# A token order kept through the gating and undone by the store: one HGRN2 attention and gated MLP kernel

## The chip, the cores and the metric

The kernel runs on one core of a Trainium2 chip. The metric is the device time in microseconds of one execution; the kernel before takes 183.43 us (median of three runs, 183.13 to 183.45). A core has five engines that run side by side, each with its own instruction queue, which it works off in order: TensorE (PE in the profile; PEld is its weight load), VectorE (DVE), ScalarE (ACT), GpSimd (POOL) and SyncE (SP). SP computes nothing here: it issues DMA transfers. The transfers of a core run on 16 DMA engines.

## The reference

Inputs are `q`, `k`, `v` and `f_logit` of shape (4 batches, 8 heads, 768 tokens, 48), and two weight matrices.

```python
f = 1.0 / (1.0 + np.exp(-f_logit))
for t in range(S):                      # 768 tokens, per batch and head a 48 x 48 state
    state = f[:, :, t, :, None] * state + np.einsum('bhd,bhe->bhde', k[:, :, t], v[:, :, t])
    y[:, :, t] = np.einsum('bhd,bhde->bhe', q[:, :, t], state)
x = y.transpose(0, 2, 1, 3).reshape(3072, 384)
h = x @ w_in                            # 384 -> 2048
g = h * np.cos(h)
out = g @ w_out                         # 2048 -> 384, written as 3072 x 384 in float32
```

The recurrence is a gated linear attention; what follows is a plain two-layer MLP whose nonlinearity is h·cos(h).

## The kernel before, in words

**Tokens.** The 3,072 tokens are cut into 12 pairs of 256 tokens (`pair(n)`). A load (`load`, L296) brings one of the four inputs of one pair, 384 KB, so that partition p holds tokens 2p and 2p+1 next to each other, for all 8 heads; the first two pairs load f, k and q in halves of 192 KB. Because of that layout the attention works on even tokens and odd tokens as two groups: in every block of 128 tokens its columns stand as 64 even tokens, then 64 odd ones. The code names the two by `e` and the place within them by `n`.

**Attention of a pair.** ACT makes the logarithm of the gate and its exponentials, PE sums them along the tokens, POOL multiplies q and k with them (`qm`, `km`, L404, the tile `qk`). The products are transposed into `qkt`: for pairs 0 to 4 on PE with a copy behind it, for pairs 5 to 11 by a DMA transpose that SP issues (`tq`, L424, two for a pair). PE then makes the scores (`sc`, L456), DVE masks them (`am`, L461, 128x1024 out of PSUM into bf16), PE forms the state (`ps`, L479) and the outputs (`y` and `yi`, L531), and ACT or DVE copies them into `x` (`xe`, L197), model dimension on the partitions, tokens in the columns, still even then odd in each 128.

**MLP.** It runs in 13 units of tokens: two of 128, then eleven of 256 (`moe(m, t0, T)`). A PSUM tile of 1,024 columns holds 8 blocks of 128 columns; PE fills it from `w_in` and `x` (`h`, L579), ACT takes the cosine into the bf16 tile `co` (L584), and DVE multiplies the two into `g` (`gate`, L561): 48 such instructions of 128x1024. `gate` reads its inputs in their order, and writes each result to the column of its token: column n of the even group goes to 2n, column n of the odd group to 2n+1, so that neighbouring results are written two elements apart. `g` thus has its columns in the order of the tokens. For each 128 tokens PE multiplies `g` with `w_out` (`o`, L595, four steps of four matmuls into one PSUM bank, `g` being the stationary operand, so that its columns become the rows of the result), ACT or DVE copies the 128x384 float32 result into one of four tiles `ot` (L197), and a store takes it to HBM (`out`, L606). There are 24 blocks: 22 stores of 192 KB, and the last two blocks (22 and 23) as two stores of 96 KB each, by columns. All are issued by SP, but for the very last, which ACT issues.

**Order.** What runs where and when is written out by hand in the string `ORDER`: each word is a step, the letter of its engine (T is PE, S ACT, V DVE, G POOL, Y SP) and the buffers that its results take; `emit` issues the steps in this order, and each engine runs its own in it. SP's queue is thus one list of loads, weight loads, transposes and stores; what stands behind a store is not issued before it. Loads of q, k, v and f have three buffers each, `ot` has four: the copy into an `ot` tile waits for the store that last read it.

The store, with its place in `moe`, is

```python
G.step(f"out{r0 // C}{cut}", ("SP", "ACT") if cut else ("SP",), lambda e, oc=oc, r0=r0, c0=c0, c1=c1: eng(
    e).dma_start(out=out[r0:r0 + C, c0:c1] if nc is not None else None, in_=oc.ap), reads=[oc])
```

where `C` is 128 and `out` is the 3072 x 384 result in HBM: partition i of `ot` goes to row r0 + i.

Of the kernel before, what the change touches and what calls it, by code (L numbers as in the profile page):

```python
# [16 lines left out]
C = 128  # L17
# [171 lines left out]
def describe(nc, cpool, ppool, q, k, v, f_logit, moe_w_in, moe_w_out, out):  # L189
# [6 lines left out]
    def copy(e, o, i):  # L196
        (nc.scalar.copy if e == "ACT" else eng(e).tensor_copy)(out=o, in_=i)  # L197
# [358 lines left out]
                e, xg[g].ap, py[g].ap[:, 0:DM].rearrange("p (m n) -> p m n", n=C)), reads=[py[g]], writes=[xg[g]])  # L556

    def gate(gv, ph, co, T):

        o = gv.ap if T == C else gv.ap.rearrange("p f (g t) -> p (f g) t", t=C)  # L560
        nc.vector.tensor_mul(out=o.rearrange("p b (n e) -> p b e n", e=2),  # L561
                             in0=ph.ap.rearrange("p (b e n) -> p b e n", e=2, n=64),
                             in1=co.ap.rearrange("p (b e n) -> p b e n", e=2, n=64))


    def moe(m, t0, T):
        n, at = divmod(t0, 2 * C)
        x, xg = xs[n]
        xw = x if T == 2 * C else xg[at // C]
        gT, F = Val(gS), 1024 // T  # L570
        for j in range(KF // F):
            ph, co = Val(p2), Val(coS)
            for s in range(2):
                def first(e, j=j, s=s, ph=ph):
                    xa = xw.ap if T == 2 * C else xw.ap[:, None]
                    for i in range(s * F // 2, (s + 1) * F // 2):
                        f0 = (j * F + i) * 128
                        for kk in range(KM):
                            nc.tensor.matmul(ph.ap[:, i * T:(i + 1) * T].rearrange("p (g t) -> p g t", t=C),  # L579
                                             lhsT=w_in_bf[:, kk, f0:f0 + 128], rhs=xa[:, :, kk, :], start=(i % (F // 2) == 0 and kk == 0),  # L580
                                             stop=((i + 1) % (F // 2) == 0 and kk == KM - 1))
                G.step(f"h{m}.{j}{s}", ("PE",), first, reads=[xw, w_in_v[(j * F + s * F // 2) // 4]],
                       writes=[ph], sums=True)
            G.step(f"co{m}.{j}", ("ACT",), lambda e, ph=ph, co=co: nc.scalar.activation(  # L584
                out=co.ap, in_=ph.ap, func=AF.Sin, bias=halfpi), reads=[ph], writes=[co], table="S")
            gv = gT.part(lambda a, j=j: a[:, j * F:(j + 1) * F, 0:T])
            G.step(f"g{m}.{j}", ("DVE",), lambda e, ph=ph, co=co, gv=gv: gate(gv, ph, co, T),
                   reads=[ph, co], writes=[gv])
        for i in range(T // C):
            po, ot = Val(p1), Val(otS)  # L590
            r0 = t0 + i * C
            for s in range(4):
                def second(e, i=i, s=s, po=po):
                    for j in range(4 * s, 4 * s + 4):
                        nc.tensor.matmul(po.ap[:, 0:DM], lhsT=gT.ap[:, j, i * C:(i + 1) * C],  # L595
                                         rhs=w_out_bf[:, j, :], start=(po.first and j == 4 * s),
                                         stop=(po.final and j == 4 * s + 3))
                G.step(f"o{r0 // C}.{s}", ("PE",), second,
                       reads=[gT.parts[4 * s // F], w_out_v[s]], writes=[po], sums=True)
            cuts = ((".0", 0, DM // 2), (".1", DM // 2, DM)) if m == len(UNITS) - 1 else (("", 0, DM),)  # L600
            for cut, c0, c1 in cuts:
                oc = ot.part(lambda a, c0=c0, c1=c1: a[:, c0:c1])
                G.step(f"ot{r0 // C}{cut}", ("ACT", "DVE"), lambda e, po=po, oc=oc, c0=c0, c1=c1: copy(
                    e, oc.ap, po.ap[:, c0:c1]), reads=[po], writes=[oc])
                G.step(f"out{r0 // C}{cut}", ("SP", "ACT") if cut else ("SP",), lambda e, oc=oc, r0=r0, c0=c0, c1=c1: eng(
                    e).dma_start(out=out[r0:r0 + C, c0:c1] if nc is not None else None, in_=oc.ap), reads=[oc])  # L606

    for n in range(PAIRS):
        pair(n)
# [1 line left out]
    for m, T in enumerate(UNITS):  # L611
        moe(m, t0, T)
        t0 += T
# [104 lines left out]
```

## Time and profile before

| | |
|---|---|
| median of 3 runs | 183.43 us (183.13 to 183.45) |
| profiled execution | 183.05 us, of which the span of instructions is 181.3 us |
| granted TensorE clock | 0.998 of full speed |
| PE busy | 174.0 us (96% of the span) |
| DVE, ACT, POOL busy | 138.2, 130.7, 109.2 us |
| DMA | 33.93 MB in 72,282 packets |

The span is counted from the first to the last instruction; all places in time below are microseconds from its start. "Busy" is the time in which an engine executes. The DMA rows count packets (a packet is one piece that one of the 16 engines moves), and the share of the 16 engines' time that the packets took. The row of a DMA issue gives the time from SP's issue to the landing of the data. The chain of work that ended last is followed back from the last instruction, at each step to what released it.

### The profile page before, as it was taken

Reading aid. Unit: us, or ns where it says so; the run is one execution under the profiler, and the core shown is the slowest. Engines: PE = TensorE matmul, PEld = TensorE weight load, DVE = VectorE, ACT = ScalarE, POOL = GpSimd, SP = SyncE. Lnnn points to the kernel's source line nnn. Section 1 sums busy time; section 2 is a strip of 40 time slices with the busy share of each in tenths; the row PEclk is TensorE's granted clock in tenths of the full one; section 3 lists DMA queues with packets and bytes.
Section 4 is the critical chain, followed back from the end, with each engine's and each line's share of the span. In section 5 each row is a group of like instructions: output and inputs, shape, how many; then the busy total and the mean of one; then the engine's idle time right before and its main releaser. Section 6 shows DMA issues by size and latency. Waiting matters only on the chain.

```text
span 181.3 us, 5818 instructions
## 1 busy us (share of the span) xinstructions
PE 174.0 (96%) x2464; PEld 124.2 (69%) x2464; DVE 138.2 (76%) x206; ACT 130.7 (72%) x187; POOL 109.2 (60%) x139
## 2 busy tenths in 40 slices
PE   7999788999999999999999999999999999999992
PEld 2555357785677876778657886658788767786661
DVE  5359988898685989897999698689888994466260
ACT  3985988778877999989997899769768452473221
POOL 4229889999969996989755968790799000000000
PEclk9999999999999999999999999999999999999999
DMA  6999999999999945996889999749929400110313
GB/s 141 261 261 263 346 304 318 293 283 281 317 264 241 270 77 128 253 230 133 125 162 317 189 242 253 175 125 244 216 85 197 90 4 0 38 52 4 130 43 130
DMA packets 72282, 33.93 MB, mean 187 GB/s; under 512 B 65344, under 2 KB 70720, under 8 KB 72256
## 3 DMA queue, kind: packets, MB, share of 16 engines
q1 hardware_dynamic: 71584, 33.27, 76.6%
q8 instruction: 19, 0.31, 0.7%
q10 hardware_dynamic: 672, 0.30, 0.6%
q14 instruction: 7, 0.06, 0.1%
HBM read 25.17 MB, written 4.72 MB: 165 GB/s over the span
## 4 chain that ended last, share of the span: by engine, by line
PE 80%; DMA 8%; SPq 5%; DVE 3%; POOL 1%; issue 1%; ACT 1%; POOLq 0%
PE ps L595 35%; PE ps L579 32%; DMA k<-in_k_dram 5%; PE ps L531 5%; SPq L296 3%; PE ps L456 3%; DMA v<-in_v_dram 3%; PE ps L479 2%; DVE g L561 1%; SPq L282 1%; PE ps L435 1%; PE ps L374 1%; DVE am L461 1%; POOL qk L404 1%; POOL k L351 1%
## 5 line engine op out<-in xcount | busy, mean ns | idle before, releaser
L561 DVE TENSOR_TENSOR g<-ps,co 128x1024 bf16<-128x1024 f32 x48 | 61.3, 1311 | 15.8 <-ACT co L584 14.8
L595 PE MATMUL ps<-w_out_bf,g 128*128 128x384 bf16 x384 | 68.9, 326 | 0.0
L579 PE MATMUL ps<-x,w_in_bf 128*128 128x256 bf16 (+1 forms) x624 | 68.2, 264 | 0.6 <-DVE x L197 0.5
L584 ACT ACTIVATE co<-ps,halfpi 128x1024 bf16<-128x1024 f32 x48 | 52.7, 1113 | 20.0 <-PE ps L579 19.8
L579 PEld LDWEIGHTS <-w_in_bf 128*128 128x128 bf16 x624 | 56.3, 98 | 9.3 <-DVE x L197 0.7
L595 PEld LDWEIGHTS <-g 128*128 128x128 bf16 x384 | 36.0, 98 | 21.5 <-issue 0.3
L461 DVE TENSOR_TENSOR am<-ps,pmask 128x1024 bf16<-128x1024 f32 x24 | 28.7, 1218 | 5.0 <-PE ps L456 4.8
L404 POOL TENSOR_TENSOR qk<-k,bi 128x384 bf16<-128x384 f32 x22 | 22.0, 1010 | 5.4 <-ACT bi L391 4.7
L404 POOL TENSOR_TENSOR qk<-q,b 128x384 bf16<-128x384 f32 x21 | 20.9, 1004 | 2.7 <-DVE q L338 2.1
L197 POOL COPY vt<-vb 64x384 bf16<-64x384 bf16 x33 | 16.7, 507 | 1.6
L264 PE MATMUL ps<-zero 128*128 128x512 bf16 x54 | 16.1, 426 | 1.2 <-DVE zero L203 1.2
L503 DVE TENSOR_TENSOR sz<-ps,b 64x192 bf16<-64x192 f32 x40 | 14.1, 353 | 2.5 <-PE ps L479 1.6
L341 POOL TENSOR_TENSOR q<-f,q 128x384 f32<-128x384 f32 x10 | 10.0, 1000 | 8.3 <-DMA q<-in_q_dram 6.1
L363 POOL TENSOR_TENSOR sp<-ls 128x384 bf16<-128x384 f32 x10 | 10.2, 1015 | 7.7 <-ACT ls L333 5.9
L329 ACT ACTIVATE f<-f 128x768 f32<-128x768 f32 (+1 forms) x14 | 10.4, 746 | 4.5 <-DMA f<-in_f_logit_dram 4.4
L351 POOL TENSOR_TENSOR k<-k,f 128x384 f32<-128x384 f32 (+1 forms) x12 | 11.1, 930 | 4.2 <-DMA k<-in_k_dram 4.2
L497 DVE TENSOR_TENSOR ps<-ps,sz 64x192 f32<-64x192 f32 x32 | 11.7, 366 | 1.9 <-PE ps L479 0.8
L197 ACT COPY ot<-ps 128x384 f32<-128x384 f32 (+1 forms) x14 | 6.1, 453 | 8.7 <-PE ps L595 8.7
L197 ACT CAST x<-ps 128x384 bf16<-128x384 f32 x12 | 5.5, 479 | 5.9 <-PE ps L531 5.9
L456 PE MATMUL ps<-qkt 48*64 48x128 bf16 (+1 forms) x304 | 8.7, 219 | 1.0 <-DVE sz L503 0.8
L197 DVE CAST x<-ps 128x384 bf16<-128x384 f32 x12 | 6.4, 552 | 4.0 <-PE ps L531 3.8
L264 PEld LDWEIGHTS <-zero 128*128 128x128 bf16 x54 | 4.9, 105 | 6.1 <-issue 2.2
(64 smaller groups left out, 167.5 us busy)
## 6 DMA issues: line engine op xcount, KB each, us to landing
v<-in_v_dram SPq DMA_DIRECT2D x12, 384.0 KB, 6.0
out_dram<-ot SPq DMA_DIRECT2D x22, 192.0 KB, 2.1
f<-in_f_logit_dram SPq DMA_DIRECT2D x10, 384.0 KB, 6.0
k<-in_k_dram SPq DMA_DIRECT2D x10, 384.0 KB, 6.7
q<-in_q_dram SPq DMA_DIRECT2D x10, 384.0 KB, 6.7
g<-in_moe_w_in_dram SPq DMA_DIRECT2D x4, 768.0 KB, 7.6
g<-in_moe_w_out_dram SPq DMA_DIRECT2D x4, 768.0 KB, 5.8
k<-in_k_dram SPq DMA_DIRECT2D x4, 192.0 KB, 4.5
```

Of the source, the lines that this page charges most:

```text
L197: (nc.scalar.copy if e == "ACT" else eng(e).tensor_copy)(out=o, in_=i)
L264: G.step(f"zf{i}", ("PE",), lambda e, dump=dump: nc.tensor.matmul(dump.ap, lhsT=zero[:, 0:128], rhs=zero, start=True, stop=True), writes=[ ...
L351: eng(e).tensor_mul(out=w.ap[:, :, 0, :], in0=w.ap[:, :, 0, :], in1=t.ap[:, :, 0, :])
L404: G.step(f"{nm}{n}.{u}", ("POOL", "DVE") if cut else ("POOL",), lambda e, u=u, j=j, src=src, dec=dec: eng(e).tensor_mul(out=qkp[u][j].ap[: ...
L456: nc.tensor.matmul(o[t0:t1, r, 2 * a + g, :].rearrange("p (e n) -> p e n", e=2), lhsT=wide[s, t0 // 64, :] if turned else wide[s].rearrang ...
L461: G.step(f"am{n}.{u}", ("DVE",), lambda e, u=u, sc=sc: nc.vector.tensor_mul(out=am[u].ap.rearrange("p r b n -> p (r b) n"), in0=sc.ap.rear ...
L497: nc.vector.tensor_add(out=view()[s], in0=view()[s], in1=S0.ap[s, :, r, :])
L503: eng(e).tensor_mul(out=new.ap[s, :, r, :].rearrange("p (u a) n -> p u a n", u=2), in0=view()[s].rearrange("p (u a) n -> p u a n", u=2), i ...
L561: nc.vector.tensor_mul(out=o.rearrange("p b (n e) -> p b e n", e=2), in0=ph.ap.rearrange("p (b e n) -> p b e n", e=2, n=64), in1=co.ap.rea ...
L579: nc.tensor.matmul(ph.ap[:, i * T:(i + 1) * T].rearrange("p (g t) -> p g t", t=C), lhsT=w_in_bf[:, kk, f0:f0 + 128], rhs=xa[:, :, kk, :], ...
L584: G.step(f"co{m}.{j}", ("ACT",), lambda e, ph=ph, co=co: nc.scalar.activation(out=co.ap, in_=ph.ap, func=AF.Sin, bias=halfpi), reads=[ph], ...
L595: nc.tensor.matmul(po.ap[:, 0:DM], lhsT=gT.ap[:, j, i * C:(i + 1) * C], rhs=w_out_bf[:, j, :], start=(po.first and j == 4 * s), stop=(po.f ...
```

## The change

The gating no longer reorders: it writes its columns in the order in which it reads them, so that `g` holds, in each block of 128 columns, 64 even tokens and then 64 odd ones. The rows of `o`, and the partitions of `ot`, then stand in that order, and the store puts them in place: partition 64·e + n of `ot` goes to row r0 + 2n + e. Its destination is written as a pattern of three dimensions, two groups of 64 rows, each row two rows on from the last. The order of the steps, their engines and their buffers are the same.

```diff
     def gate(gv, ph, co, T):
-
-        o = gv.ap if T == C else gv.ap.rearrange("p f (g t) -> p (f g) t", t=C)
-        nc.vector.tensor_mul(out=o.rearrange("p b (n e) -> p b e n", e=2),
-                             in0=ph.ap.rearrange("p (b e n) -> p b e n", e=2, n=64),
-                             in1=co.ap.rearrange("p (b e n) -> p b e n", e=2, n=64))
+        nc.vector.tensor_mul(out=gv.ap if T == C else gv.ap.rearrange("p f (g t) -> p (f g) t", t=C),
+                             in0=ph.ap.rearrange("p (b t) -> p b t", t=C), in1=co.ap.rearrange("p (b t) -> p b t", t=C))
...
                 G.step(f"out{r0 // C}{cut}", ("SP", "ACT") if cut else ("SP",), lambda e, oc=oc, r0=r0, c0=c0, c1=c1: eng(
-                    e).dma_start(out=out[r0:r0 + C, c0:c1] if nc is not None else None, in_=oc.ap), reads=[oc])
+                    e).dma_start(out=out[r0:r0 + C, c0:c1].rearrange("(n e) m -> e n m", e=2) if nc is not None else None, in_=oc.ap), reads=[oc])
```

In the built program one thing changes on DVE's list of instructions, the output pattern of the 48 gates, and one on SP's and ACT's, the destination of the stores (the line numbers move by three):

```
-L606 DMACopy out_dram<-ot_155 128x384
+L603 DMACopy out_dram<-ot_155 2x64x384
...
-L606 DMACopy out_dram<-ot_154 128x192
+L603 DMACopy out_dram<-ot_154 2x64x192
```

## The prediction

> **What bounds the kernel now.** I read the page first (busy shares, DMA, chain), then the windows, which split the span where the loads end.
>
> ```profile
> span 181.3 us, 5818 instructions
> ...
> PE 174.0 (96%) x2464; PEld 124.2 (69%) x2464; DVE 138.2 (76%) x206; ACT 130.7 (72%) x187; POOL 109.2 (60%) x139
> ...
> DMA  6999999999999945996889999749929400110313
> ...
> q1 hardware_dynamic: 71584, 33.27, 76.6%
> ...
> PE 80%; DMA 8%; SPq 5%; DVE 3%; POOL 1%; issue 1%; ACT 1%; POOLq 0%
> ```
>
> ```profile
> core 0: us, PE busy (x) PEld busy (x) DVE busy (x) ACT busy (x) POOL busy (x), PEclk, DMA share, GB/s
> ...
> 60.50:143.80 83.30, 83.30 (x1303) 62.74 (x1302) 72.92 (x98) 71.09 (x98) 62.45 (x78) 1.00 0.84 186
> 143.80:157.30 13.50, 13.50 (x225) 9.62 (x223) 8.91 (x11) 4.55 (x8) 0.00 (x0) 1.00 0.01 2
> 157.30:178.20 20.90, 20.71 (x150) 14.38 (x147) 10.93 (x12) 8.22 (x10) 0.00 (x0) 1.00 0.19 69
> 178.20:181.30 3.10, 0.00 (x0) 0.00 (x0) 0.00 (x0) 0.39 (x2) 0.00 (x0) 0.89 0.34 114
> ```
>
> PE is the bound: it holds 80% of the chain and is busy without a gap from 60.5 (the first store) to 157.3. But DMA is a close second: q1, which carries SP's transfers, keeps 16 engines busy for 76.6% of the span, and 0.84 of them in the stretch of 60.5 to 143.8, the last in which anything is loaded or transposed. That figure is a mean over 16 engines, and holds for each only while every transfer is dealt evenly. After 143.8 there are only stores.
>
> **The gate.** It writes contiguous results instead of results two elements apart. The nearest contiguous write is the mask `am`: same engine, size and types.
>
> ```profile
> L561 DVE TENSOR_TENSOR g<-ps,co 128x1024 bf16<-128x1024 f32 x48 | 61.3, 1311 | 15.8 <-ACT co L584 14.8
> L461 DVE TENSOR_TENSOR am<-ps,pmask 128x1024 bf16<-128x1024 f32 x24 | 28.7, 1218 | 5.0 <-PE ps L456 4.8
> ```
>
> ```profile
> 28.10 1.33 DVE g L561
> ...
> 30.64 1.23 DVE g L561
> ```
>
> So a gate saves between nothing (1311 ns stays) and 1311 − 1218 = 93 ns; I take 93, the row that differs least from what it becomes. That is 48 × 93 ns = 4.5 us of DVE, which has idle time anyway. Only two gates lie on the chain of work: −0.2 us. PE reads `g` as before, in the same blocks of 128 columns: nothing.
>
> **The store's issue.** Its pattern has one more dimension. The least a store's issue took is 0.36 us (ACT row, below), the dearest kind of issue on SP is a transpose (3.31 us for two, below). So 25 issues on SP and one on ACT may grow by between nothing and 1.3 us. On SP this hides behind the stores' own backlog; only the last issue is on the path. I take +0.3 us, near the plain store, since a store it remains.
>
> **The store's transfer.** This is where I see the cost. A view of the DMA between 157 and 160, when two stores run and nothing else:
>
> ```profile
> DMA  0000000000000003699999520000005999999400
> ...
> DMA packets 288, 0.39 MB, mean 131 GB/s; under 512 B 32, under 2 KB 288, under 8 KB 288
> ...
> q1 hardware_dynamic: 288, 0.39, 34.9%
> ...
> out_dram<-ot SPq DMA_DIRECT2D x2, 192.0 KB, 1.9
> ```
>
> Each store is 128 packets of 1,536 bytes (its rows) and 16 short ones, one for each engine. The packets take 34.9% of 16 × 3 us = 16.75 us for 393,216 bytes: 23.5 bytes per ns and engine. On 16 engines a store's 8 packets for each last 12,288 / 23.5 = 0.52 us. The rest of the 1.9 us to landing is fixed: about 0.7 us ahead (issue at 157.33, the busy digits start near 158.05) and 0.65 behind.
>
> In the changed program the destination's outermost dimension is 2, where every copy before has 128 (the instruction lists under the change). If engines are dealt along that dimension, a store has two shares of 64 rows: 98,304 / 23.5 = 4.2 us on each of two engines, 3.7 us more than now, and 2.1 us for a half store (+1.85). If the rows are dealt as before, it is nothing. No transfer of before has a short outermost dimension, so its trace doesn't say which; the 16 equal shares of today fit both. I take two, because that dimension is the one thing of the transfer that the change alters; ends for the range are 0 and 3.7 us.
>
> [...]
>
> **Stage 1, to 60.5:** no store yet; −0.2 us as said.
>
> **Stage 2, 60.5 to 143.8.** What the queue holds:
>
> ```profile
> q1 hardware_dynamic: 39907, 15.30, 83.5%
> ...
> out_dram<-ot SPq DMA_DIRECT2D x15, 192.0 KB, 3.9
> q<-in_q_dram SPq DMA_DIRECT2D x6, 384.0 KB, 5.5
> k<-in_k_dram SPq DMA_DIRECT2D x5, 384.0 KB, 5.0
> v<-in_v_dram SPq DMA_DIRECT2D x5, 384.0 KB, 6.1
> f<-in_f_logit_dram SPq DMA_DIRECT2D x4, 384.0 KB, 5.2
> qkt<-qk SPq DMA_TRANSPOSE x14, 3.3
> ```
>
> Each engine has 83.5% of 83.3 = 69.6 us of work. Part of that is crowding: all packets average 27.9 ns here, while between 115.3 and 118, a quieter moment, short ones cost 48.8% × 16 × 2.7 us / 920 = 22.9 ns:
>
> ```profile
> q1 hardware_dynamic: 920, 0.35, 48.8%
> ```
>
> At that price the (39,907 − 15 × 128) / 16 short packets of an engine are 54.4 us, with 15 × 0.52 for the stores 62 us. Fifteen stores add 15 × 3.7 = 55 us on the two engines: 117 to 125 us of work in a stretch of 83.3. The two engines become the bound, and the last transpose lands 34 to 41 us later (I take 37.5), since a load or transpose has landed only when its slowest engine is through and those two have the stores ahead of it. The engines also idle: before, 83.3 − 69.6 = 13.7 us here. Between 0 (the stores fill the gaps) and 13.7 (they stay, because SP issues in order: a load behind a store waits for PE's results, and PE for the load) I take 5. Queued behind the stores are the loads for POOL and ACT, the transposes for PE's scores, and through the four `ot` buffers PE's own banks.
>
> What the last transpose feeds is not due at once:
>
> ```profile
> 138.55 3.31 SPq L424 DMA_TRANSPOSE qkt<-qk  x2
> 157.33 21.39 SPq L606 DMA_DIRECT2D out_dram<-ot  x10
> ```
>
> ```profile
> 147.65 0.57 PE ps L456 x32
> ```
>
> The last pair's scores start at 147.65, 3.8 us after 143.8: −3.8 us.
>
> **Stage 3, the tail.** The issues of the last stores:
>
> ```profile
> 167.48 1.31 SPq L606 DMA_DIRECT2D out_dram<-ot  x3
> ```
>
> ```profile
> 175.11 3.61 SPq L606 DMA_DIRECT2D out_dram<-ot  x5
> ```
>
> ```profile
> 178.62 0.36 ACTq L606 DMA_DIRECT2D out_dram<-ot  x1
> ```
>
> On two engines the three stores of 167.48 run from 168.2 to 180.8. Block 20 needs the `ot` buffer of block 16, the last of the three: landed 181.4, copied and issued, first packet 182.7. Then two full stores and four halves, 2 × 4.2 + 4 × 2.1 = 16.8 us, to 199.5, landed at 200.1. Today the last lands at 178.62 + 1.7 = 180.3: +19.8 us.
>
> **The sum,** against the profiled execution's 183.05 us (span 181.3 and 1.75 around it; the median of the runs is 0.4 above): 183.05 − 0.2 + 37.5 + 5 − 3.8 + 19.8 + 0.3 = 241.7. I say 242.
>
> **The rivals.**
> Serial: PE's waits come on top of the stores' time instead of beside it. For it: SP's list is in order, and few buffers stand between. Price: all added store time, 22 × 3.7 + 4 × 1.85 = 89 us: 272.
> Tail alone: the loads are early enough for the stores' backlog, and only stage 3 shows: 183 + 20 = 203. Against it: 117 us of work do not fit in 83.3 us. It needs the stores to be cheaper or the stretch's loads to come much earlier.
> Rows dealt as before, on 16 engines: the change leaves the store as it is, and the gates off the path: 183, within 0.2%. For it: the bytes and rows are the same.
> Faster: the same dealing, and the gates' 4.5 us of DVE reach PE. It decides if more than 0.37 us does, four gates on the path where the chain shows two; DVE's share of the chain is 3%, so the price is at most 0.3 to 2 us: about 182.
>
> **How the numbers follow.** Two engines, overlapping: 0.70, between 222 (uncrowded packets, no idle, a cheaper tail) and 262 (crowded, all idle stays). Serial 0.10, 262 to 280. Tail alone 0.10, 200 to 222. As before 0.06. Faster 0.04. The range of 212 to 268 takes the first whole and half of its two neighbours: 0.80. A measurement of this kernel tells 0.2% from no change; slower by more than that holds 0.91 (one in a hundred for dealing as before, with dearer issues), within it 0.05, faster 0.04.
>
> **What would show it.** Gates at about 1,218 ns. A lone store's time to landing at about 5.5 us (0.7 + 4.2 + 0.65) instead of 1.9; two short packets for each store instead of 16, so 26 × 14 = 364 packets fewer in all; the DMA digits at 1 where stores run alone, though DMA is the bound. PE no longer gapless after 60.5, its waits ending with DMA; the chain's DMA share far above 8%. Stores at 2 us would prove the dealing wrong; stores at 5.5 us and PE still gapless, the queueing.

## The result, and the profile after

The changed kernel takes 240.57 us (median of six runs, 239.94 to 242.22) against 183.44 us: 1.3123 times the time before, with a 95% interval of 1.3082 to 1.3165. Ratios, here and below, leave out the runs that lie more than 1.5% above the fastest of their kernel: two of four each for `ot8` and `ot8_free_e4`, one of four for `ot8_e4`, for which the times given are those of the other runs. The profiled execution has a span of 238.2 us, 56.9 us more than before. The page of the kernel after, the lines that answer to those shown of before:

```profile
span 238.2 us, 5818 instructions
...
PE 182.3 (77%) x2464; PEld 127.6 (54%) x2464; DVE 134.5 (56%) x206; ACT 130.8 (55%) x187; POOL 109.3 (46%) x139
...
PEclk9999999999999769999999889999558999997555
DMA  7999999999753587676959585868930001010111
...
DMA packets 71918, 33.93 MB, mean 142 GB/s; under 512 B 64980, under 2 KB 70356, under 8 KB 71892
...
q1 hardware_dynamic: 71234, 33.27, 64.9%
...
DMA 35%; PE 28%; POOL 9%; issue 7%; ACT 6%; SPq 5%; DVE 4%; DVEq 0%; ACTq 0%; POOLq 0%
...
L559 DVE TENSOR_TENSOR g<-ps,co 128x1024 bf16<-128x1024 f32 x48 | 57.2, 1220 | 29.7 <-ACT co L581 28.7
```

The same bytes moved (33.93 MB), in 72,282 − 71,918 = 364 packets fewer: 14 for each of the 26 stores, as forecast with two short packets for a store instead of sixteen. The last ten DMA digits, where stores run alone, stand at 0 and 1: two engines of sixteen are an eighth. DMA has gone from 8% of the chain to 35%, PE from 80% to 28%. The digits of the granted clock, at 9 throughout before, fall to 5 in places.

The rate of the two engines is read from a view of the DMA between 203 and 218, where three stores run alone:

```profile
GB/s 0 0 0 25 12 41 20 33 37 29 41 49 49 49 53 49 49 49 49 53 49 49 49 53 49 49 49 49 53 49 49 53 49 49 49 53 49 33 0 0
DMA packets 390, 0.59 MB, mean 39 GB/s; under 512 B 6, under 2 KB 390, under 8 KB 390
...
q1 hardware_dynamic: 390, 0.59, 11.3%
```

Six short packets for three stores, two each. By the bytes moved, the first store is slow and uneven, and from then on the pair moves 49 to 53 GB/s, by which a store of 196,608 bytes takes 3.9 us. The packets' share gives more: 11.3% of 16 × 15 us = 27.1 us for 589,824 bytes, 21.7 bytes per ns and engine, or 4.5 us for a store. It adds up the packets' times, and packets of one engine overlap: between 209.32 and 213.24, from the end of the first store's packets to the end of the second's, the view shows 13.3% of 16 × 3.92 us = 8.3 us of packet time for two engines, 4.2 us each, within 3.92 us.

```profile
DMA packets 130, 0.20 MB, mean 50 GB/s; under 512 B 2, under 2 KB 130, under 8 KB 130
...
q1 hardware_dynamic: 130, 0.20, 13.3%
```

Where the 56.9 us came from is read at one place in PE's order, the scores of the last pair, the first work on the last transposes. The timeline of PE, before and then after (start, length):

```profile
147.58 0.64 PE L456 MATMUL ps<-qkt 48*64 48x128 bf16 x32
```

```profile
182.33 0.64 PE L456 MATMUL ps<-qkt 48*64 48x128 bf16 x32
```

They start 34.75 us later; the first store is issued at 60.6, as before. From there to the end it is 55.9 us against 33.7: +22.2 us. The longest pieces of the chain of waits in the first of these stretches (60 to 182.4; start, length, what):

```profile
71.49 10.01 DMA out_dram<-ot
102.35 10.45 DMA out_dram<-ot
116.71 7.92 DMA f<-in_f_logit_dram
141.37 7.79 DMA v<-in_v_dram
164.32 11.43 DMA out_dram<-ot
```

Before, this stretch of the chain (60 to 147.7) was all PE:

```profile
by line: PE ps L579 43.4%; PE ps L595 39.6%; PE ps L531 6.6%; PE ps L456 4.5%; PE ps L479 3.0%; PE ps L374 1.5%; PE ps L435 1.0%; PE ps L380 0.5%
```

Now it holds 47.6 us of transfers in five pieces: three stores, and two loads that took 7.9 and 7.8 us to land, where the medians of this stretch were 5.2 and 6.1 before.

### The profile page after: what moved, and what is told of

Same layout as the page of the kernel before. It is cut to its first block, busy times and chain, and to the rows that moved or that the text cites. A ratio compares the mean times of both kernels' runs of the same rounds, so it can differ in the third digit from the quotient of the medians.

```text
span 238.2 us, 5818 instructions
## 1 busy us (share of the span) xinstructions
PE 182.3 (77%) x2464; PEld 127.6 (54%) x2464; DVE 134.5 (56%) x206; ACT 130.8 (55%) x187; POOL 109.3 (46%) x139
## 2 busy tenths in 40 slices
DMA packets 71918, 33.93 MB, mean 142 GB/s; under 512 B 64980, under 2 KB 70356, under 8 KB 71892
## 4 chain that ended last, share of the span: by engine, by line
DMA 35%; PE 28%; POOL 9%; issue 7%; ACT 6%; SPq 5%; DVE 4%; DVEq 0%; ACTq 0%; POOLq 0%
DMA out_dram<-ot 26%; PE ps L576 12%; PE ps L592 11%; DMA v<-in_v_dram 6%; DMA f<-in_f_logit_dram 3%; SPq L296 3%; POOL qk L404 2%; ACT co L581 2%; PE ps L531 2%; POOL vt L197 2%; SPq L603 2%; ACT f L329 1%; POOL sp L363 1%; POOL k L351 1%; ACT ls L333 1%
## 5 line engine op out<-in xcount | busy, mean ns | idle before, releaser
L592 PE MATMUL ps<-w_out_bf,g 128*128 128x384 bf16 x384 | 71.5, 335 | 6.3 <-ACT ot L197 4.3
L559 DVE TENSOR_TENSOR g<-ps,co 128x1024 bf16<-128x1024 f32 x48 | 57.2, 1220 | 29.7 <-ACT co L581 28.7
L576 PE MATMUL ps<-x,w_in_bf 128*128 128x256 bf16 (+1 forms) x624 | 71.9, 272 | 1.8 <-ACT ot L197 1.2
L576 PEld LDWEIGHTS <-w_in_bf 128*128 128x128 bf16 x624 | 58.1, 101 | 12.3 <-issue 2.0
L592 PEld LDWEIGHTS <-g 128*128 128x128 bf16 x384 | 36.9, 100 | 30.1 <-issue 8.2
L461 DVE TENSOR_TENSOR am<-ps,pmask 128x1024 bf16<-128x1024 f32 x24 | 28.7, 1218 | 11.6 <-PE ps L456 11.4
L197 ACT COPY ot<-ps 128x384 f32<-128x384 f32 (+1 forms) x14 | 6.1, 453 | 47.9 <-DMA out_dram<-ot 47.1
L456 PE MATMUL ps<-qkt 48*64 48x128 bf16 (+1 forms) x304 | 9.2, 224 | 14.2 <-DMA qkt<-qk 9.0
L456 PEld LDWEIGHTS <-qkt 48*64 48x64 bf16 (+1 forms) x304 | 6.2, 106 | 17.7 <-DMA qkt<-qk 11.9
L197 DVE COPY ot<-ps 128x384 f32<-128x384 f32 (+1 forms) x12 | 5.8, 518 | 14.9 <-DMA out_dram<-ot 14.1
L479 PE MATMUL ps<-vb,qk 64*64 64x48 bf16 x320 | 6.2, 194 | 5.1 <-ACT bi L395 5.0
```

Source lines behind the costliest of these rows:

```text
L456: nc.tensor.matmul(o[t0:t1, r, 2 * a + g, :].rearrange("p (e n) -> p e n", e=2), lhsT=wide[s, t0 // 64, :] if turned else wide[s].rearrang ...
L461: G.step(f"am{n}.{u}", ("DVE",), lambda e, u=u, sc=sc: nc.vector.tensor_mul(out=am[u].ap.rearrange("p r b n -> p (r b) n"), in0=sc.ap.rear ...
L559: nc.vector.tensor_mul(out=gv.ap if T == C else gv.ap.rearrange("p f (g t) -> p (f g) t", t=C), in0=ph.ap.rearrange("p (b t) -> p b t", t= ...
```

## The experiments

Ratios are to the kernel before, run beside each on the same chip (medians of 183.1 to 183.5 us).

**The two halves of the change, each alone.** `gate_alone`:

```diff
 (after)
-   e).dma_start(out=out[r0:r0 + C, c0:c1].rearrange("(n e) m -> e n m", e=2) ..., in_=oc.ap)
+   e).dma_start(out=out[r0:r0 + C, c0:c1] ..., in_=oc.ap)
```

> The gate writes its columns as it reads them, the store is that of before, so the rows of the result stay in even-then-odd order in HBM. Theory (the cost is the store's alone): gates at 1,220 ns, PE's chain as before, 183.0 to 183.5 us. Rival (the gate's columns cost PE something): over 184 us. Rival (the gates' 4.5 us of DVE reach PE): under 182.5 us.

Measured: 183.0 us, ratio 0.9989 (0.9976 to 1.0001). The gates take 1,219 ns. `store_alone` is the reverse, the gate of before with the store of after:

```diff
 (before)
-   e).dma_start(out=out[r0:r0 + C, c0:c1] ..., in_=oc.ap)
+   e).dma_start(out=out[r0:r0 + C, c0:c1].rearrange("(n e) m -> e n m", e=2) ..., in_=oc.ap)
```

> The gate of before, the store of after, so the rows of the result are permuted. Theory (the store on two engines is the whole cost): 240 to 242 us, as after, with 71,918 DMA packets. Rival (the gate has a part in it): clearly below 240 us.

Measured: 240.84 us, ratio 1.3154 (1.3111 to 1.3196). The whole cost is the store's; what the gate saves, if anything, is at the edge of what the runs tell.

**How many groups.** `store_e16`, `store_e8` and `store_e4` keep the three-dimensional pattern and rows that are apart, and change only the number of groups:

```diff
 (after)
-   ... .rearrange("(n e) m -> e n m", e=2) ...
+   ... .rearrange("(n e) m -> e n m", e=16) ...     # and 8, 4
```

> The kernel after with the destination cut into 16 groups of 8 rows instead of 2 groups of 64: three dimensions and rows that are apart, as after, but an outermost dimension of 16; the rows of the result come out in another order. Theory (the outermost dimension sets the number of engines): 16 engines, 16 short packets a store, 72,282 in all, a lone store lands in about 1.9 us, 183 to 185 us. Rival (the form of the pattern makes the store dear, three dimensions or rows apart, on however many engines): about 240 us.

> The kernel after with 4 groups of 32 rows; the rows of the result come out in another order. Theory: four engines, 2.1 us of a store on each, 26 x 12 = 312 packets fewer than before (71,970). In the middle stretch 15 x 1.6 = 24 us more on four engines: 86 to 93 us of work in 83.3, and a tail of +4.6 us: 187 to 198 us, likeliest 191. Rival (form of the pattern): about 240 us. Rival (time is added in proportion to what a store takes longer, 1.57 of 3.7 us, 42% of 57 us): about 207 us.

> The kernel after with 8 groups of 16 rows (the rows come out in another order): eight engines, 1.05 us of a store on each, half a microsecond more than on sixteen. Sixteen groups cost 1.5 us, four 26.6, two 57. If time grows in proportion to a store's time on its engine (0.52 us more, at about 15.6 us a microsecond, and the 1.5 of the form): 190 to 194 us. If there is a threshold, as the prediction's sum has it (62 to 70 + 15 x 0.52 = 70 to 78 us of work fit in 83, only the tail's 1 to 2 us and the form's 1.5 show): 185 to 188 us.

Measured; a short packet is one under 512 bytes, and "to the last scores" is the start of the PE row shown above against the kernel before:

| groups | packets fewer than before | per store | us | ratio (95%) | to the last scores | from there on |
|---|---|---|---|---|---|---|
| 16 | 0 | 0 | 184.56 | 1.0074 (1.0052 to 1.0096) | +0.97 | +0.5 |
| 8 | 208 | 8 | 187.85 | 1.0265 (1.0224 to 1.0307) | +2.2 | +2.2 |
| 4 | 312 | 12 | 209.75 | 1.146 (1.1428 to 1.1492) | +17.7 | +8.4 |
| 2 (after) | 364 | 14 | 240.57 | 1.3123 (1.3082 to 1.3165) | +34.75 | +22.2 |

A store leaves as many short packets as it has groups: 16 − 8, 16 − 4 and 16 − 2 of them are missing from each. I take their count for the count of engines, since the highest rate in views with these stores goes with it: 53 GB/s with 2 groups (203 to 218), 103 with 4 (185 to 194.5), 215 with 8 (170 to 178), 378 with 16 (165 to 178), 24 to 27 for each. The pattern's form costs 1.5 us, not 57: the rival of the form falls. Between 8 and 4 groups lies the threshold that the sum of the engines' work puts there, and the 187.85 us lie in the range that went with it, outside that of a cost in proportion (190 to 194). With 4 the time lies 12 us above the range of the same sum, and 3 above the rival's estimate by proportion. A view of the DMA of the four-group kernel between 185 and 194.5, with three stores:

```profile
GB/s 0 0 0 0 0 6 52 19 13 13 39 45 71 78 97 103 103 103 97 97 91 97 103 97 103 97 103 97 97 103 78 103 97 97 91 65 26 0 0 0
...
q1 hardware_dynamic: 396, 0.59, 19.3%
```

Again the first store is slow; then the four engines move about 97 to 103 GB/s, twice what the two do, by which a store takes 2.0 us, where I had put 2.1. (By the packets' share, 19.3% of 16 × 9.5 us = 29.3 us for 589,824 bytes, it would be 2.4 us.)

**The tail alone.** `store_tail` has the new destination only in the eleven stores issued after the last transpose:

```diff
 (before)
-   e).dma_start(out=out[r0:r0 + C, c0:c1] ...
+   e).dma_start(out=(out[r0:r0 + C, c0:c1].rearrange("(n e) m -> e n m", e=2)
+                     if r0 // C >= 15 else out[r0:r0 + C, c0:c1]) ...
```

> The kernel before, in which only the stores of blocks 15 to 23 (all those that are issued after the last transpose, and none ahead of it) have the new destination; the rows of these blocks come out in another order. Theory: the stretch with loads is as before, the tail grows by the prediction's 20 us: 202 to 206 us. Rival (the tail's cost in after was made by what came before it): under 198 us.

Measured: 205.47 us, ratio 1.1205 (1.1183 to 1.1226), +21.9 us. The last scores start at 147.87, as before. The longest pieces of the chain from 150 to the end, first of this kernel, then the same three of after (176 to 238.2):

```profile
158.71 9.46 DMA out_dram<-ot
169.87 13.29 DMA out_dram<-ot
183.84 6.57 DMA out_dram<-ot
```

```profile
193.18 9.32 DMA out_dram<-ot
...
204.21 13.29 DMA out_dram<-ot
...
218.18 6.57 DMA out_dram<-ot
```

They are the same to 0.15 us: the tail costs its 22 us whatever came ahead of it, and the two stretches add up. The last of the three pieces is a store that starts with no other store under way: it lands 6.57 us after its issue, where the prediction's sign was 5.5 and a store took 1.9 before.

**Do the four `ot` buffers hold PE?** The longest waits of after:

```profile
ACT ot L197 <- DMA out_dram<-ot: 47.1, 6, 16.5
...
DVE ot L197 <- DMA out_dram<-ot: 14.1, 4, 8.0
```

61 us of copies waiting for a store to free their buffer (total, times, longest). `ot8_free` has eight buffers:

```diff
 (after)
-         ... "ot": 4}
+         ... "ot": 8}
+    free = list(range(8))
 ...
                 v.slot = places.pop(0)
+                if v.pool.name == "ot":
+                    v.slot = free.pop(0)
 ...
+        if s.name.startswith("out") and not s.name.endswith(".0"):
+            free.append(s.reads[0].whole.slot)
```

> The kernel after with eight ot buffers, each taken when the store of its last block stands ahead in the order (in the run ot8 the store of block 2 stood behind the copy of block 8 into the same buffer and sent that block's rows). Theory (the two engines and SP's order hold the stretch, the buffers don't): 230 to 240 us. Rival (the buffers couple PE to the stores): 205 to 225 us.

Measured: 231.32 us, ratio 1.2602 (1.255 to 1.2655). The waits for stores are gone from the list, and others have grown. The longest of the chain in the middle stretch (60 to 176.3):

```profile
72.61 5.84 SPq L296
95.43 6.98 DMA qkt<-qk
108.11 7.87 PE ps L576 x72
116.59 7.79 DMA f<-in_f_logit_dram
141.09 7.78 DMA v<-in_v_dram
```

From 71.5 on, the chain of after waited for a store; now it has SP standing for 5.8 us in the issue of a load behind two stores. The buffers are worth 9 of 57 us. Two further runs share a flaw: they take the eight buffers strictly in turn, so that the store of block 2 stands behind the copy of block 8 into the same buffer and sends block 8's rows in place of its own. `ot8`:

```diff
+                if v.pool.name == "ot":
+                    v.slot, n_ot = n_ot % 8, n_ot + 1
```

> The kernel after with eight ot buffers, taken in turn, instead of four; nothing else. In after, ACT waits 47 us and DVE 14 us for a store to free such a buffer. Theory of the prediction (the two engines' work is the bound: 117 us in the stretch from the first store to the last transpose, which took 118): the waits vanish but others take their place, 234 to 241 us. Rival (PE's waits come on top of the stores because of the few buffers): 205 to 225 us.

Its ratio was 1.2663 (1.2625 to 1.2702), near that of `ot8_free`. `ot8_e4` is the same with `e=4`:

> Eight ot buffers and stores in 4 groups of 32 rows (the rows come out in another order): the run on four engines took 209.8 us where 86 to 93 us of work in 83 gave 191. Theory (there the bound is not the engines' work but a store's time to landing, through the four buffers): most of the difference goes, 190 to 200 us. Rival (SP's list in order is what couples them, not the buffers): 206 to 210 us.

It took 204.1 us, ratio 1.11 (1.1043 to 1.1157). `ot8_free_e4`, `ot8_free` with `e=4`, puts that right:

> The same eight buffers with stores in 4 groups (the rows come out in another order), against 209.8 us with four buffers. Buffers as the coupling: 190 to 198 us. SP's order as the coupling (a load stands behind stores): 202 to 209 us.

Measured: 203.8 us, ratio 1.1115 (1.1025 to 1.1204), 6 us under the four-group kernel. With four engines too, the buffers are the smaller part, 6 of 27 us: the 190 to 198 us that went with them as the coupling do not hold, nor the 190 to 200 of `ot8_e4`.

**Is it SP's order?** `act_stores` moves the stores to ACT's queue:

```diff
 (after)
+        if name.startswith("out"):
+            how = "S"
         plan.append((G.steps[name], LETTER[how[0]], ...
```

> The kernel after with all stores issued by ACT at the same places of the order, so that they are in ACT's DMA queue, and no load or transpose stands behind them in SP's; still two groups, so two engines. If loads and transposes queued behind stores in SP's list are what holds the middle stretch: it shrinks from +35 us to +5 to +20, the tail stays at +22: 212 to 228 us. If not (the two engines' time or the four ot buffers hold it): 233 to 245 us. ACT may lose time of its own to waits for DVE's copies, which would push it to the upper end of either.

Measured: 253.79 us, ratio 1.3842 (1.3803 to 1.3881), above both ranges. The longest waits:

```profile
ACT ot L197 <- DMA out_dram<-ot: 63.7, 7, 15.3
DVE g L559 <- ACT co L581: 43.8, 18, 13.1
```

Loads no longer stand behind stores in a list, and still it is slower. But ACT, which also makes the cosines, now waits longer for buffers (63.7 us against 47.1), and the gates wait for it (43.8 us against 28.7). The last scores start at 190.66, 43.1 us later than before, and the rest adds 28.0. So the run does not tell what SP's order alone is worth.

**A version in order on sixteen engines.** `split_parity` keeps the gate of after and issues each store as two:

```diff
 (after)
-   ... eng(
-   e).dma_start(out=out[r0:r0 + C, c0:c1].rearrange("(n e) m -> e n m", e=2) ..., in_=oc.ap) ...
+   def put(e, ...):
+       rows = out[r0:r0 + C, c0:c1].rearrange("(n e) m -> e n m", e=2)
+       for x in range(2):
+           eng(e).dma_start(out=rows[x], in_=oc.ap[64 * x:64 * x + 64])
 ...
```

> The gate of after, and each store issued as two: the 64 partitions of even tokens to every second row, then the 64 of the odd ones. Destination and source have 64 as outermost dimension; the result is in order. Theory (64 is dealt to 16 engines): 16 short packets for each of 52 stores, 26 x 16 = 416 more than before (72,698), 183 to 185.5 us, the more by what SP's 26 further issues cost. Rival (half the partitions use half the engines): 8 short packets each and 190 to 200 us.

Measured: 187.74 us, 2 us over my range, ratio 1.0245 (1.0211 to 1.0279), with 72,698 packets, 416 more: 16 short ones for each of 52 stores. It takes back 53 of the 57 us, but loses 2 us by the last scores (149.61) and 2 in the tail. SP's list has 25 more issues of 0.59 us (median), and each packet takes longer. Between 158 and 164, with two blocks stored alone:

```profile
DMA packets 320, 0.39 MB, mean 66 GB/s; under 512 B 64, under 2 KB 320, under 8 KB 320
...
q1 hardware_dynamic: 320, 0.39, 27.2%
```

27.2% of 16 × 6 us = 26.1 us for 393,216 bytes: 15 bytes per ns of packet time, where the whole store of before has 23.5. How the 4 us divide between the two was not separated. No version here that leaves the rows in order beats the kernel before.

## Why the prediction was right

**The dealing: shown by the counts and the rates.** Two groups, two engines, by the rates given with the table of groups. The packets fell by exactly 364. Stores of 2, 4, 8 and 16 groups leave 2, 4, 8 and 16 short packets, those of 64 rows in `split_parity` and of 128 rows in the kernel before leave 16, and with 16 groups the cost all but vanishes (184.56 us). That all stores meet on the same two engines, as the prediction's 55 us of added work, and with it its 117 to 125, assume, no run shows: the traces have no row by engine. What they show in its place is that three stores one behind another (203 to 218) never exceed 53 GB/s together, where with four groups three reach 103, and that the stretch from the first store to the last packet of the transposes took 116.7 us.

**The gate: right.** 1,218 ns were forecast, 1,220 measured; 0.2 us on the path, and `gate_alone` has 0.1 to 0.2 us less with an interval that just reaches no change.

**The tail: right, 2 us low.** Forecast +19.8 (+0.3 of issue), measured +22.2 in after and +21.9 alone. The buffer of block 16 did hold block 20 (the 13.29 us piece). The transfer itself was slightly overrated, 4.2 us where a store behind another takes 3.9. Too low was what the first store after a pause costs: 6.57 us to landing instead of 5.5, and such a pause comes three times. (The 0.7 us ahead of a store's packets are 0.8 by the digits on which they rest, which start at 158.1.) The three stores before the last pause are also issued 0.85 us later after the last scores than before (20.75 instead of 19.90 us), since a copy waited for the two stores ahead of them (the 9.32 us piece).

**The middle: the mechanism borne out in the main, the number partly luck.** Forecast 37.5 + 5 − 3.8 = 38.7, measured 34.75. The last packet of the transposes ends at 177.3 instead of 143.3, 34.0 us later. Windows of before and then of after; the columns are the stretch, its length, the busy times of PE, PEld, DVE, ACT and POOL, PE's granted clock, the DMA share and GB/s:

```profile
142.50:143.20 0.70, 0.70 (x21) 0.62 (x15) 0.39 (x2) 0.70 (x2) 0.00 (x0) 1.00 1.00 186
143.30:147.50 4.20, 4.20 (x80) 2.87 (x78) 4.12 (x5) 2.19 (x4) 0.00 (x0) 1.00 0.00 0
```

```profile
70.60:72.00 1.40, 1.40 (x17) 0.88 (x18) 1.37 (x3) 1.40 (x3) 1.05 (x2) 1.00 0.00 0
134.60:136.00 1.40, 1.09 (x38) 0.83 (x38) 0.33 (x1) 0.26 (x1) 1.26 (x3) 0.84 0.00 0
156.00:157.20 1.20, 1.20 (x13) 1.08 (x12) 1.04 (x2) 1.10 (x2) 1.20 (x2) 1.00 0.00 0
...
176.30:177.20 0.90, 0.84 (x3) 0.40 (x3) 0.00 (x0) 0.88 (x3) 0.00 (x0) 0.50 1.18 231
177.30:182.30 5.00, 5.00 (x76) 3.06 (x74) 1.85 (x3) 2.10 (x3) 0.00 (x0) 0.74 0.00 0
```

Two terms were wrong, in opposite directions. Work and idle time together were to add 42.5 us, and added 34.0. The idle time was not too high: in the 116.7 us from the first store to 177.3 no engine has a packet in these three gaps and in three shorter ones, at least 5.2 us in all, so that the two engines' work is 111.5 us at most. The forecast's 117 to 125 was too much, since it took packet times for engine time, and they overlap: between 176.3 and 177.2 the share of the 16 engines comes to 1.18. The other term is the −3.8 us of slack, which did not come: PE is busy for all 5.0 us between the last packet and the last scores, at a clock of 0.74, with work that it had not done while it waited, and the chain comes to the scores from a store (164.32 in the list above), not from a transpose. The scores moved 0.75 us more than the transposes, not 3.8 less: 8.5 us too much and 4.55 too little leave the 4 us.

That the two engines' work is what fills this stretch is supported by three things: a threshold between 8 groups (70 to 78 us of work, which fit in 83.3) and 4; the length of the stretch, of which 111.5 us at most were work, near the 54 + 15 × 3.9 = 113 of the lower price; and that freeing the buffers mostly brought other waits forward. It is not shown directly, since the trace has no row by engine.

**With four groups the sum fails.** Its 187 to 198 us had no idle time in them. The last packet of the transposes ends there at 158.3, 98 us after the first store and 15.0 later than before, where 86 to 93 us of work were forecast; 4.5 us of the 98 are without any packet. The scores come 2.7 us later still instead of 3.8 earlier, and the tail costs 8.4 us instead of 4.6.

```profile
158.30:165.30 7.00, 7.00 (x83) 4.15 (x81) 4.56 (x6) 2.10 (x3) 0.00 (x0) 0.65 0.00 0
```

From four groups to two, a store's time on its engines grows by 1.9 us, 15 stores' by 29; the stretch grows by 19. So the engines' work alone does not set it with four groups. What does, how much idle time stays, and SP's part in it are open, since `act_stores` changed two things at once.

**The form: mis-sized.** I took 0.3 us for the last issue; `store_e16` shows 1.5 us in all. An issue of the new form takes 0.54 us at least, against 0.33:

```profile
L606 SPq DMA_DIRECT2D out_dram<-ot x25: 332/419/2553, 60.5 to 178.4; - x25
```

```profile
L603 SPq DMA_DIRECT2D out_dram<-ot x25: 538/584/1494, 59.9 to 179.4; - x25
```

(minimum, median and maximum in ns; the kernel before, then the one with 16 groups). That the 242 came out 1.4 us from 240.57 is partly luck, since errors offset each other: 4 us too much in the middle (itself the rest of two larger errors) and 2 too little in the tail. The form's cost and that of PE's slower clock (182.3 us busy instead of 174.0 for the same instructions), for which the prediction has no term, are contained in both.

**The rivals.** The tail alone (203) is what `store_tail` measures (205.47), and after has 35 us more; the serial one's 272 lies 31 us above what was measured. "Rows dealt as before" falls with the packet count, and "faster" with the time.

## What to carry to other kernels

Before a DMA's pattern is rearranged, look at its outermost dimension: here a store of 128 rows that was written as 2 × 64 left 2 short packets instead of 16, took 3.9 us behind another store and 6.57 us to landing when it stood alone, where a store of before landed in 1.9, and the kernel lost 57 us with the same 33.93 MB to move. The busy share averaged over 16 engines hid this, with digits of 0 and 1 in the tail that these stores held up; the short packets of a store, 2, 4, 8 and 16 for as many groups, showed it. Where a share of packet time is used as an engine's work, compare it with the time between first and last packet: here it gave 4.2 us for a store that took 3.92. Reordering that an engine with idle time does within an instruction it runs anyway (here 91 ns in a gate) was cheaper than each of the ways tried here to have the store do it.

## What the runs showed of the hardware that was not expected

**PE's clock fell when PE waited.** Windows of after, columns as above:

```profile
60.60:78.00 17.40, 16.88 (x272) 12.46 (x270) 15.27 (x22) 13.69 (x20) 15.13 (x20) 1.00 0.52 121
78.00:90.00 12.00, 7.55 (x120) 5.54 (x120) 5.53 (x10) 7.20 (x10) 5.83 (x7) 0.72 0.71 171
82.50:86.00 3.50, 3.50 (x47) 2.59 (x47) 2.12 (x4) 2.52 (x3) 1.65 (x2) 0.50 0.93 240
...
161.00:179.00 18.00, 8.14 (x84) 5.24 (x83) 6.36 (x7) 3.17 (x5) 3.74 (x5) 0.65 0.76 75
```

After PE's first stall behind a store (77.5 to 82.45) the granted clock (third column from the end) is 0.50 of full speed, and 24 matmuls of L576 take 5.03 us that take 2.73 us in the kernel before. From the chain of each, after and before, at the same place in PE's order:

```profile
83.08 5.03 PE ps L576 x24
```

```profile
78.02 2.73 PE ps L579 x24
```

PE's busy time rose from 174.0 to 182.3 us for the same instructions. So PE's waits cost more here than their length; how much of the 8.3 us lies on the path was not separated. The first stall lasted 4.97 us, the clock stood at 0.50 behind it (82.5 to 86), and over the 71 us from 90 on it is back at 0.98; from 161 to 179, where PE is busy for 8.14 of 18 us, it is 0.65. What sets it was not tried. The prediction left it out.

**Packets of one engine overlap, so their share is not its rate.** By the share of packet time, rows of 1,536 bytes that run alone come to 23.5 bytes per ns with neighbouring rows on 16 engines, 21.7 with two engines, 20.1 with four, and 15 with 64 partitions on 16 engines. By the bytes moved, two and four engines are alike once one store stands behind another: 49 to 53 and 97 to 103 GB/s, 24 to 27 per engine. Why a packet takes longer in some patterns, and why the first store after a pause is slow, was not tried.
